# Chunk 0 of a gated attention + token-MLP kernel: V ahead of k and q, with the gate weights loaded from ScalarE's queue

## The chip, the cores and the metric

The kernel runs on one core of a Trainium2 chip. The metric is the device time of one execution in microseconds (us), as the median of several runs. Five engines work side by side, each on its own in-order list of instructions: TensorE (PE, matmuls), VectorE (DVE), ScalarE (ACT), GpSimd (POOL) and SyncE (SP, which here only starts transfers). An instruction that waits holds up everything behind it on its engine.

## The reference

One input `x` (2048 tokens x 448) goes through two branches whose results are mixed by a gate per token:

```
g = sigmoid((x * gate_w).sum(-1, keepdims=True))
a = attention(x)      # 16 heads of 28; 4 segments of 512 tokens
b = token_mlp(x)      # layernorm over 448, then mixing over the 2048 tokens
return g * a + (1 - g) * b
```

The attention branch computes `q = x @ wq`, `k = x @ wk`, `v = x @ wv`, masked softmax attention inside each of the four segments, and a linear-attention memory that each segment reads from the segments before it (`num = phi(q) @ M`, `den = phi(q) @ z`, then `M += phi(k).T @ v`). The two are mixed per head by `sigmoid(beta)` and multiplied by `wo`. The MLP branch normalizes each token, and computes `u = gelu(w1.T @ h + b1)` over tokens (2048 to 1792) and `y = w2.T @ u + b2` (1792 to 2048).

## The kernel before

**Tiling.** The 2048 tokens are 16 tiles of 128, and 4 chunks of 512 (chunk = segment). The 448 input columns are three blocks of 128 and a rest of 64. q and k of a chunk are computed transposed, in 4 head groups (`hg`) of 128 rows by 512 tokens; q and k of one head group need three matmuls of a 128-row block each (`kf`, `qf`, line 608; for chunk 0 of k one at a time, `kc`, line 618) and one of the 64-row rest (`l`, `l2`, `l3`, line 627). V is computed per token tile, with x as the stationary operand and the 448 columns of `wv` moving; a 449th column holds the gate weights, so that the gate's logits come out of V's matmuls. A tile's V is three matmuls (`vf`, line 694) and one of the rest (`vl`, `vl2`, line 706). `sc` is the scores of one fill (line 838), `exp` the softmax's exponential on ACT (line 848), `pv` the product with V (line 879). `u.f.t` is one matmul of the first MLP layer: feature tile f of 14, token tile t of 16 (line 994); `y.T.f` one of the second (line 1047); `wo` the output projection (line 1020).

**Order.** The whole order of work is written out in `PLAN` (lines 31 to 113): each item is `name.arguments@engine` and, where it has one, a buffer or PSUM bank. The items are recorded in that order, each engine's list being the items with its letter (P, A, D, G, S). A recorder (`Sched`) gives every instruction a wait on the last instruction that wrote what it reads, or that still reads what it overwrites. Nothing is reordered after that.

**Chunk 0's inputs.** `ldx.0` and `ldx.1` load the first four token tiles. Chunk 0's transposed x is made on PE (`trx`, line 552), from `ldx` and a small copy of the last 64 columns (`xw`); its results are copied out of PSUM by `ex` (line 561). Chunks 1 to 3 get their transposed x straight from DRAM (`xtd`, two transposing transfers each, lines 420 and 421) with a small copy behind it (`xtc`). Weights are loaded by `ldwk` (four transfers), `ldwq` (two) and `ldwv` (two), all on SP's queue. `pad` copies k's and q's weights into head slots of 32 columns; `rid` fills the spare columns with parts of q. `ldgw` loads the gate weights, `btg` transposes them on PE, `gcp` copies them into V's extra column in three small copies on DVE. `wvc` copies the 64-row rest of `wv`.

**Evacuation.** PSUM has 8 banks. Chunk 0's k and q are copied out by `ek` and `eq`, V by `ev` (all through `copy`, lines 367 to 371, on ACT or DVE), and the gate's logits by `gt` on ACT.

**The MLP's inputs.** Each token tile is normalized before it can be used in `u`: `bn` (statistics, DVE, line 948), `lnc` (a group of four tiles' scale and shift, ten small POOL instructions), `lna` (apply, DVE line 983 or ACT line 980). Tiles 8 to 11 come with the transfer `ldx.3`, tiles 12 to 15 with `ldx.4`. `w1` and `w2` come in 15 transfers `ldr.0` to `ldr.14` into a ring of three slots; `ldr.0` serves `u.0` and `u.1`, `ldr.2` serves `u.4` and `u.5`.

**Other transfers on SP.** `pkt` transposes the memory branch's phi(k), `gw` and `gr` send the parts of q that rode in k's spare rows through DRAM to their place; `gr` of a chunk waits for `gw` of the same chunk; `ldsm` loads the biases and beta (three transfers).

**Around the change.** Before, the recorded start is: k's weights, q's weights, V's weights, gate weights, then `xtd.1`, `ldx.2`, `xtd.2`, `ldsm`, `ldr.0`, `ldx.3`, `ldx.4`, `ldr.1`, `xtd.3` on SP; on PE twelve `kc`, then `qf` and the rests, and V of chunk 0 (`vf.0` to `vf.3`, `vl2`) after that, mixed with V of chunk 1's first half (`vl.2`, `vf.4`, `vf.5`). `l3.3` is the first PE item that needs chunk 3's transposed x.

Of the kernel before, what the change touches and what calls it, by code (L numbers as in the profile page):

```python
# [30 lines left out]
warm@P acttab@A dve0@D id@G ldx.0@S ldx.1@S mz@G ldwk.0@S ldwk.1@S ldwk.2@S ldwq@S trx.0.0@P0 xw.0@A trx.0.2@P1  # L31
trx.0.3@P xw.1@A trx.0.1@P trx.1.0@P2 ldwk.6@S trx.1.2@P3 ex.0.0@D trx.1.1@P trx.1.3@P fill@P ex.0.1@D ex.1.0@A ldwv@S
ex.1.1@A bn.3@D pad.k.0@D pad.k.1@D kc.0.3@P0 ldgw@S kc.0.2@P1 kc.1.2@P pad.k.2@D xtd.1@S kc.0.1@P0 kc.0.0@P1 kc.1.3@P
kc.1.0@P kc.1.1@P pad.q.1@D kc.2.2@P bn.2@D kc.2.0@P kc.2.1@P kc.2.3@P pad.l.1@D bn.1@D qf.0.2@P2 pad.q.0@D qf.0.3@P3
wvc@D ldx.2@S pad.l.0@D bn.0@D l2.1@P xtd.2@S qf.0.1@P2 lnc.0@G eq.0.2@A ek.0.3@D ek.0.2@A btg@P2 qf.0.0@P3 gcp@D
l2.0@P xtc.1@D pkm.0.1@D0 vl.2@P01 vf.5@P ek.0.1@A eq.0.0@D eq.0.1@A rid.q@D vf.3@P0 ev.5@A ldsm@S vf.1@P3 rid.k@D
ek.0.0@A oz@G vf.4@P rid.3@A bn.4@D ldr.0@S0 vf.0@P2 ev.4@A bn.6@D ldx.3@S vf.2@P1 bn.7@D gt.2@A eq.0.3@A vl2@P
lna.0@D l.1.2@P20 l.1.0@P13 ev.0@A ev.1@D kf.1.2@P ldx.4@S ev.2@A bn.5@D ev.3@A kf.1.0@P lna.1@D lnc.1@G gt.0@A
ek.1.2@D gt.1@A qf.1.0@P ek.1.0@A ldr.1@S1 xtc.2@D sc.0.0@P eq.1.0@D xtd.3@S l3.2@P21 exp.0.0@A0 kf.2.3@P lna.2@D
qf.1.2@P ek.2.3@D kf.1.3@P eq.1.2@D pke.0.1@A0 l.2.1@P31 ek.1.3@D sc.0.1@P kf.2.1@P lna.3@D exp.0.1@A1 pkm.0.0@D1  # L40
l.2.0@P02 bn.10@D kf.2.0@P bn.9@D qf.2.1@P bn.8@D ek.2.0@A mask.0.1@G bn.13@D qf.2.0@P eq.2.1@A bn.11@D sc.0.2@P
ek.2.1@A l.1.1@P01 eq.2.0@D lnc.2@G tb@A qf.1.1@P exp.0.2@A2 lna.4@D lna.6@D u.0.0@P3 u.0.1@P bn.14@D u.0.2@P u.0.3@P
u.1.0@P2 lna.5@D u.1.1@P lna.7@A bn.12@D u.1.2@P u.1.3@P kf.1.1@P bn.15@D pke.0.0@A1 u.0.4@P eq.1.1@D u.0.5@P u.1.4@P
ek.1.1@A u.0.6@P pkn.0.0@D u.1.5@P u.0.7@P lnc.3@G lna.8@A u.1.6@P u.1.7@P xtc.3@D pkt.0.0@S0 sc.0.3@P lna.10@D btr@P1
l3.3@P0 exp.0.3@A3 b1c@D lna.11@D u.1.8@P kf.3.3@P lna.9@D pkt.0.1@S b2c@D u.0.8@P u.0.9@P ek.3.3@D u.0.10@P u.1.9@P
u.0.11@P pkn.0.1@D sc.0.4@P vl.6@P10 exp.0.4@A4 vf.12@P pkt.0.3@S mask.0.3@G lna.12@D vf.13@P lna.13@D u.1.10@P
pkt.0.2@S ev.12@D u.0.12@P u.1.11@P ev.13@A u.0.13@P mask.0.4@G lna.14@D u.1.12@P u.1.13@P gt.6@A sc.1.0@P lna.15@A
gw.1@S l.3.1@P01 mask.0.0@G kf.3.1@P exp.1.0@A5 u.1.14@P mask.0.2@G u.1.15@P u.0.14@P qf.3.1@P eu.1@D ek.3.1@A
u.0.15@P sc.1.1@P eq.3.1@D eu.0@A pv.0@P20 ldr.2@S2 ldr.3@S0 pv.1@P01 exp.1.1@A0 ta.0@D l.3.0@P13 bet@D qf.3.0@P
u.2.0@P2 u.2.1@P u.2.2@P eq.3.0@D gr.1@S u.2.3@P sc.1.2@P kf.3.0@P pkm.1.1@D1 exp.1.2@A1 pkm.1.0@D0 u.3.0@P3 u.2.4@P  # L50
ek.3.0@D u.2.5@P u.3.1@P u.3.2@P pqm.1.0@D0 u.2.6@P u.2.7@P nr.0@D pke.1.0@A1 u.2.8@P ta.1@D sc.1.3@P mst.0@P1
exp.1.3@A2 u.3.3@P u.2.9@P msa.0@D u.2.10@P u.2.11@P u.3.4@P oa.0@D0 u.3.5@P vl.3@P01 mask.1.3@G sc.1.4@P vf.7@P
exp.1.4@A3 mask.1.2@G u.2.12@P vf.6@P ev.7@D mask.1.0@G u.3.6@P u.2.13@P ev.6@D u.2.14@P mask.1.1@G u.3.7@P u.2.15@P
gt.3@A sc.2.0@P eu.2@D l.3.2@P01 exp.2.0@A4 qf.3.2@P mask.1.4@G u.4.0@P2 u.3.8@P eq.3.2@D u.3.9@P u.3.10@P kf.3.2@P
# [193 lines left out]
def build_kernel(nc, X, WQ, WK, WV, WO, BETA, W1, B1, W2, B2, GW, OUT):  # L248
# [143 lines left out]
    def ldwv(eng, u):  # L392
        dma(eng, wvx[:, 0:3, 0:D], full3(WV), writes=[R_wv], group="wv")
        dma(eng, wvx[half[1], 3, 0:D], WV[384:448, :], writes=[R_wv], group="wv")

    def wvc(eng, u):
        copy(eng, wvx[half[0], 3, 0:D], wvx[half[1], 3, 0:D], [R_wv], [R_wv6])
# [287 lines left out]
    def vf(eng, u, t):  # L685
        tc = t // 4
        if tc == 0:
            slot["v", t] = u[0]
# [445 lines left out]
```

## Time and profile before

| | |
|---|---|
| median of 7 runs | 176.76 us (176.38 to 177.25) |
| profiled execution, its own time | 176.62 us |
| span of its trace | 174.9 us, 3285 instructions |
| PE busy | 167.5 us (96% of the span) |
| DVE, ACT, POOL busy | 133.4, 121.2, 54.3 us |
| DMA | 24.01 MB, mean 137 GB/s |
| 224 `u` and 238 `y` matmul records | 49.2 and 47.3 us |
| 40 `exp` on ACT | 75.1 us, 1877 ns each |

The profile is one execution recorded by the hardware. Starts are in us from the beginning of the span. A row's time is from its start to its modelled end; matmuls overlap, so that matmuls of 448 columns that take 353 ns by the mean start 189 ns apart. The time outside the span is 176.62 - 174.9 = 1.72 us.

### The profile page before, as it was taken

To read this page: it belongs to the slowest core of one execution; us is meant where nothing else is said; L and a number is where in the kernel's file an instruction comes from. 1 tells how busy PE (TensorE), PEld (TensorE's weight loads), DVE (VectorE), ACT (ScalarE), POOL (GpSimd) and SP (SyncE) were. 2 spreads that over 40 slices of the span, in tenths; PEclk is the share of its full clock that TensorE was granted. 3 is DMA by queue.
4 is the path that set the end of the run, shared out by engine and by line. 5 is a ranking of instruction groups with operands and counts; after the bars stand their busy time and mean duration, and the time that the engine had idled before them with its cause. 6 is when DMAs were issued, how large, how long until landed. Compare 5 with 4: busy or idle time off the path is not lost.

```text
span 174.9 us, 3285 instructions
## 1 busy us (share of the span) xinstructions
PE 167.5 (96%) x1286; PEld 78.5 (45%) x1302; DVE 133.4 (76%) x276; ACT 121.2 (69%) x113; POOL 54.3 (31%) x100
## 2 busy tenths in 40 slices
PE   7799999899999999999999999999999999999994
PEld 3334334344544444544444445444444444455563
DVE  3789969876757884899599476899998979996113
ACT  4239899688878788878997979995787774600300
POOL 7044534872075046320400009123108252200000
PEclk9999999999999999999999999999999999999999
DMA  5987999243950398189791542600727268291022
GB/s 139 261 179 155 267 340 181 60 84 83 307 146 4 47 240 105 22 223 222 193 236 27 151 95 59 185 0 0 222 72 210 74 183 225 71 250 43 2 67 64
DMA packets 49456, 24.01 MB, mean 137 GB/s; under 512 B 14337, under 2 KB 49441, under 8 KB 49441
## 3 DMA queue, kind: packets, MB, share of 16 engines
q1 hardware_dynamic: 49441, 23.81, 55.6%
q8 instruction: 10, 0.16, 0.4%
q14 instruction: 5, 0.04, 0.1%
HBM read 18.48 MB, written 2.18 MB: 118 GB/s over the span
## 4 chain that ended last, share of the span: by engine, by line
PE 76%; SPq 9%; DMA 7%; DVE 5%; issue 2%
PE t L1047 24%; PE t L994 23%; SPq L361 9%; DMA t<-in_A_x_dram 7%; PE t L1020 7%; PE t L838 6%; PE t L879 5%; PE t L694 3%; PE t L608 3%; PE t L803 2%; DVE t L948 2%; PE t L706 1%; DVE t L1005 1%; PE t L627 1%; DVE t L1056 1%
## 5 line engine op out<-in xcount | busy, mean ns | idle before, releaser
L848 ACT ACTIVATE t<-t 128x2048 bf16<-128x2048 f32 x40 | 75.1, 1877 | 20.0 <-PE t L838 19.6
L861 POOL TENSOR_SCALAR_AFFINE_SELECT t<-t 128x1024 bf16<-128x1024 bf16 (+1 forms) x40 | 37.4, 954 | 82.2 <-ACT t L848 82.2
L994 PE MATMUL t<-t 128*128 128x448 bf16 x224 | 49.2, 353 | 0.5 <-DVE t L371 0.2
L1047 PE MATMUL t<-t 128*128 128x448 bf16 (+1 forms) x238 | 47.3, 342 | 0.2 <-issue 0.2
L1047 PEld LDWEIGHTS t<-t 128*128 128x128 bf16 x238 | 22.1, 98 | 19.4 <-issue 2.8
L994 PEld LDWEIGHTS t<-t 128*128 128x128 bf16 x224 | 20.9, 98 | 22.0 <-issue 2.3
L371 DVE CAST t<-t 128x512 bf16<-128x512 f32 (+1 forms) x23 | 15.3, 670 | 6.6 <-PE t L608 4.6
L369 ACT ACTIVATE t<-t 128x512 bf16<-128x512 f32 (+5 forms) x28 | 13.9, 533 | 8.6 <-PE t L627 5.9
L1056 DVE SCALAR_TENSOR_TENSOR t<-t 128x448 bf16<-128x448 f32 (+1 forms) x17 | 10.8, 648 | 11.3 <-PE t L1047 11.2
L608 PE MATMUL t<-t 128*128 128x512 bf16 x68 | 18.0, 380 | 0.7 <-issue 0.2
L838 PE MATMUL t<-t 28*128 28x512 bf16 (+3 forms) x256 | 15.8, 301 | 0.1
L1030 ACT ACTIVATE t<-t 128x448 bf16<-128x448 f32 x9 | 6.3, 721 | 12.0 <-PE t L1020 12.0
L1020 PE MATMUL t<-t 128*128 128x448 bf16 x64 | 14.2, 352 | 0.1
L1005 DVE TENSOR_SCALAR t<-t 128x448 bf16<-128x448 f32 x12 | 8.2, 682 | 5.8 <-PE t L994 5.7
L757 ACT ACTIVATE t<-t 128x1024 bf16<-128x1024 bf16 x12 | 12.6, 1050 | 0.0
L899 DVE STREAM_TRANSPOSE t<-t 128x512 f32<-128x512 f32 x16 | 11.1, 696 | 1.3 <-PE t L879 1.3
L940 DVE STREAM_TRANSPOSE t<-t 128x512 bf16<-128x512 bf16 x16 | 10.8, 686 | 0.1
L920 DVE SCALAR_TENSOR_TENSOR t<-t 128x448 bf16<-128x448 f32 x16 | 10.7, 686 | 0.1
L838 PEld LDWEIGHTS t<-t 28*128 28x128 bf16 x256 | 4.5, 92 | 13.9 <-issue 7.1
L694 PE MATMUL t<-t 128*128 128x449 bf16 x48 | 10.7, 354 | 0.0
L948 DVE BATCH_NORM_STATS2 t<-t 128x6 f32<-128x448 bf16 x16 | 9.3, 615 | 1.4 <-DMA t<-in_A_x_dram 1.4
L879 PE MATMUL t<-t 128*32 128x512 bf16 (+3 forms) x256 | 10.3, 301 | 0.0
(77 smaller groups left out, 155.0 us busy)
## 6 DMA issues: line engine op xcount, KB each, us to landing
t<-in_B_w_dram SPq DMA_DIRECT2D x7, 1024.0 KB, 7.9
t<-in_B_w_dram SPq DMA_DIRECT2D x8, 896.0 KB, 5.3
out_dram<-t SPq DMA_DIRECT2D x15, 112.0 KB, 1.8
t<-in_A_x_dram SPq DMA_DIRECT2D x3, 448.0 KB, 7.9
t<-in_A_x_dram SPq DMA_DIRECT2D x2, 224.0 KB, 2.7
t<-in_A_wo_dram SPq DMA_DIRECT2D x4, 98.0 KB
t<-in_A_wk_dram SPq DMA_DIRECT2D x3, 112.0 KB, 3.4
t<-in_A_wq_dram SPq DMA_DIRECT2D x1, 336.0 KB, 3.3
```

The source lines that it names most:

```text
L361: op(eng, lambda e: e.dma_start(out, in_, transpose=True) if transpose else e.dma_start(out, in_), reads=reads, writes=writes, dma=True, g ...
L369: op("ACT", lambda e: e.activation(out, in_, ACT.Copy), reads=reads, writes=writes)
L371: op(eng, lambda e: e.tensor_copy(out, in_), reads=reads, writes=writes)
L608: m = e.matmul(bank(b)[:, 0:512], wkq[:, c0 + c, 128 * hg : 128 * hg + 128], xTb[:, tc % NXT, c, :], start=first and c == 0, stop=last and ...
L694: m = e.matmul(bank(b)[:, 0 : D + 1], xTb[:, tc % NXT, c, k0 : k0 + 128], wvx[:, c, 0 : D + 1], start=tc == 0 and c == 0, stop=tc > 0 and ...
L838: last = e.matmul(bank(hl)[:, c0 : c0 + w], kT[r, hg, s * 512 + j * 128 : s * 512 + j * 128 + 128], qT[r, hg, s * 512 + 128 * j : s * 512 ...
L848: op("ACT", lambda e: e.activation(punit(i).rearrange("p (a q) -> p a q", a=4), ps[:, 0:4, :], ACT.Exp, scale=SCALE), reads=R_bank[0:4], w ...
L861: op("POOL", lambda e: e.affine_select(d, d, pattern=pat, compare_op=ALU.is_ge, fill=0.0, base=0, channel_multiplier=-1), reads=[R_P[i]], ...
L879: last = e.matmul(bank(b)[32 * hl : 32 * hl + 32, 128 * j : 512], vaug[:, 4 * s + j, 32 * h : 32 * h + 32], p4[:, hl, c0 : c0 + w], start= ...
L994: op("PE", lambda e: e.matmul(bank(b)[:, 0:D], w[:, st, (ft % 2) * 128 : (ft % 2) * 128 + 128], xtile(st)[:, 0, :], start=(st == 0), stop= ...
L1020: last = e.matmul(bank(b)[:, 0:D], oT[:, hg, T * 128 : T * 128 + 128], wo_sb[:, hg, :], start=(hg == 0), stop=(hg == NHG - 1), skip_group_ ...
L1047: op("PE", lambda e, b=b, f=f, c0=c0, n=n: e.matmul(bank(b)[:, 0:n], w[:, f, c : c + 128], uT[:, f, c0 : c0 + n], start=(f == 0), stop=(f ...
```

## The change

`PLAN` is written anew from the first to the last line, and the functions are adapted to its new start. The computation is the same, with the same matmuls.

- On PE, chunk 0 starts with V by blocks: twelve `vc` (block c of token tile t) and `vl2`; then k's twelve `kc`, and q's `qf`. `btg` stands ahead of `trx`.
- V of chunk 0 goes to PSUM banks 0 to 3, and q of chunk 0 later to the same banks (`qf` takes `u[0]`, k always a bank from 4 on), so q's matmuls come behind V's evacuation.
- `ldwv` becomes four transfers of their own, recorded ahead of `ldwk` and `ldwq`; each block of `wv` has its own resource.
- `ldgw` moves from SP's queue to ACT's.
- Among the items whose engine changes at the start: `xw.0` from ACT to DVE, `ex.0.1` from DVE to ACT, `ex.1.0` and `ex.1.1` from ACT to DVE, `pad.q.0` from DVE to ACT, `xtc.1` from DVE to ACT. `gcp` stands ahead of `ex` on DVE.
- The rest of the plan is in another order too; for the items that the prediction speaks of, the lines are below.

```diff
 PLAN = """
-warm@P acttab@A dve0@D id@G ldx.0@S ldx.1@S mz@G ldwk.0@S ldwk.1@S ldwk.2@S ldwq@S trx.0.0@P0 xw.0@A trx.0.2@P1
-trx.0.3@P xw.1@A trx.0.1@P trx.1.0@P2 ldwk.6@S trx.1.2@P3 ex.0.0@D trx.1.1@P trx.1.3@P fill@P ex.0.1@D ex.1.0@A ldwv@S
-ex.1.1@A bn.3@D pad.k.0@D pad.k.1@D kc.0.3@P0 ldgw@S kc.0.2@P1 kc.1.2@P pad.k.2@D xtd.1@S kc.0.1@P0 kc.0.0@P1 kc.1.3@P
...
+warm@P ldgw@A dve0@D id@G ldx.0@S ldx.1@S acttab@A mz@G ldwv.0@S ldwv.1@S ldwv.2@S ldwv.6@S btg@P0 trx.0.2@P1 gcp@D
+trx.0.0@P2 ldwk.0@S trx.0.1@P xw.1@A xw.0@D ldwk.1@S trx.0.3@P ex.0.0@D trx.1.2@P3 trx.1.0@P0 ldwk.2@S ex.0.1@A
+trx.1.1@P trx.1.3@P fill@P ex.1.0@D ldwq@S vc.0.0@P0 ex.1.1@D vc.0.1@P1 vc.0.2@P2 bn.3@D vc.1.2@P vc.0.3@P3 ldwk.6@S
+bn.1@D vc.1.3@P vc.1.0@P vc.2.3@P wvc@D xtd.1@S vc.1.1@P vc.2.0@P pad.k.0@D vc.2.1@P vc.2.2@P pad.k.1@D vl2@P
+kc.0.0@P2 pad.k.2@D ev.3@A kc.0.3@P1 kc.1.0@P kc.0.2@P0 pad.q.0@A pad.q.1@D kc.0.1@P3 ev.2@D kc.1.1@P kc.1.2@P
+kc.1.3@P ev.0@D ldx.2@S kc.2.1@P gt.1@A kc.2.2@P pad.l.1@D kc.2.3@P ev.1@D xtd.2@S rid.3@A qf.0.3@P2 bn.2@D gt.0@A
+kc.2.0@P qf.0.2@P3 bn.0@D l2.1@P lnc.0@G qf.0.1@P0 ek.0.2@A ek.0.3@D xtc.1@A qf.0.0@P1 pad.l.0@D eq.0.3@D l2.0@P
+eq.0.2@D ldsm@S vl.2@P01 vf.5@P ek.0.0@A rid.k@D ek.0.1@A vf.4@P rid.q@D ldr.0@S0 ev.5@A ldx.3@S eq.0.0@A pkm.0.1@D0
+l.1.1@P23 bn.7@D ev.4@A kf.1.1@P eq.0.1@A bn.5@D qf.1.1@P gt.2@A bn.6@D lna.1@A ldx.4@S sc.0.0@P lna.3@D ek.1.1@A
+l.1.2@P01 xtc.2@D pkm.0.0@D1 kf.1.2@P tb@A eq.1.1@A bn.4@D ldr.1@S1 qf.1.2@P pke.0.0@A0 ek.1.2@D lnc.1@G xtd.3@S
+l.2.1@P23 lna.2@D qf.2.1@P exp.0.0@A0 lna.0@D eq.1.2@D kf.2.1@P pkn.0.0@D l3.2@P01 kf.1.3@P eq.2.1@D ek.2.1@A kf.2.3@P
+bn.11@D ek.1.3@A u.0.0@P2 bn.8@D mask.0.0@G u.0.1@P ek.2.3@A sc.0.1@P bn.10@D l.1.0@P30 exp.0.1@A1 btr@P1 bn.9@D
+qf.1.0@P b1c@D bn.15@D lnc.2@G kf.1.0@P lna.4@D u.0.2@P b2c@D lna.6@D u.0.3@P ek.1.0@A u.0.4@P eq.1.0@D u.1.0@P1
+pke.0.1@A1 u.1.1@P u.1.2@P bn.12@D u.1.3@P sc.0.2@P bn.13@D l.2.0@P30 exp.0.2@A2 u.1.4@P lna.7@D kf.2.0@P bn.14@D
+qf.2.0@P lna.5@D pkt.0.0@S0 lnc.3@G lna.8@D u.0.5@P pkn.0.1@D u.1.5@P eq.2.0@A u.0.6@P u.1.6@P lna.9@D gw.1@S ek.2.0@A
+u.0.7@P u.1.7@P u.1.8@P xtc.3@D sc.0.3@P lna.11@D l3.3@P0 gc.0@D exp.0.3@A3 u.0.8@P kf.3.3@P pqm.1.0@D0 lna.10@D
...
+u.2.3@P u.2.4@P u.2.5@P pke.1.0@A0 u.2.6@P u.2.7@P sc.1.3@P l.3.0@P21 exp.1.3@A2 qf.3.0@P pkn.1.0@D pkm.1.1@D0 u.3.4@P
+pkt.1.0@S1 u.3.5@P u.3.6@P kf.3.0@P pke.1.1@A1 mask.1.3@G u.3.7@P gr.1@S sc.1.4@P ek.3.0@D mask.1.2@G u.2.8@P
+exp.1.4@A3 u.2.9@P eq.3.0@D u.3.8@P u.3.9@P u.2.10@P msc.0@D mask.1.0@G u.2.11@P u.2.12@P ldr.2@S2 u.3.10@P u.3.11@P
...
 """
...
-    def ldwv(eng, u):
-        dma(eng, wvx[:, 0:3, 0:D], full3(WV), writes=[R_wv], group="wv")
-        dma(eng, wvx[half[1], 3, 0:D], WV[384:448, :], writes=[R_wv], group="wv")
+    def ldwv(eng, u, j):
+        if j == 6:
+            dma(eng, wvx[half[1], 3, 0:D], WV[384:448, :], writes=[R_wvu])
+            return
+        dma(eng, wvx[:, j, 0:D], WV[128 * j : 128 * j + 128, :], writes=[R_wv[j]])
...
-            slot["k", 0, hg] = u[0] if early(0, hg) else 4 + u[0]
+            slot["k", 0, hg] = 4 + u[0]
...
-            slot["q", tc, hg] = u[0] if early(tc, hg) else 4 + u[0]
+            slot["q", tc, hg] = u[0]
...
+    def vc(eng, u, c, t):
+        if c == 0:
+            slot["v", t] = u[0]
+        b = slot["v", t]
+        op("PE", lambda e: e.matmul(bank(b)[:, 0 : D + 1], xTb[:, 0, c, 128 * t : 128 * t + 128], wvx[:, c, 0 : D + 1],
+                                    start=c == 0, stop=False, skip_group_check=True),
+           reads=[R_xT[0][2 * (t // 2) + c // 2], R_wv[c], R_gw], writes=[R_bank[b]])
```

`vf` loses its branch for chunk 0.

## The prediction

> **What bounds the kernel now.** I read the engine shares first, then the busy time by stretch, then the chain of waits up to 34 us, then SP's timeline and the waits of PE.
>
> ```profile
> PE 167.5 (96%) x1286; PEld 78.5 (45%) x1302; DVE 133.4 (76%) x276; ACT 121.2 (69%) x113; POOL 54.3 (31%) x100
> ...
> PEclk9999999999999999999999999999999999999999
> ```
> ```profile
> 16.00:33.00 17.00, 15.68 (x95) 5.96 (x95) 15.14 (x32) 13.89 (x20) 8.05 (x24) 1.00 0.91 211
> 33.00:60.00 27.00, 26.37 (x240) 12.08 (x244) 19.78 (x42) 22.54 (x19) 11.28 (x18) 1.00 0.47 110
> 60.00:172.00 112.00, 111.31 (x882) 54.59 (x890) 86.77 (x171) 77.37 (x61) 27.54 (x29) 1.00 0.50 125
> ```
> Columns of the second: stretch, length, busy PE, weight loads, DVE, ACT, POOL, clock, DMA share, GB/s. From 33 us on PE is busy in 137.7 of 139 us, at full clock: there the time is PE's work, and it is the same work in the new kernel. What can change is when PE gets past the start. In 16 to 33 us the DMA engines are at 0.91 and DVE at 15.1 of 17.
>
> ```profile
> 16.53 8.72 DMA t<-in_A_x_dram
> 25.27 2.73 DVE t L948 x5
> 28.00 0.60 DVE t L371
> 28.61 0.07 SPq L361
> 28.71 3.71 DMA t<-in_A_x_dram
> 32.42 0.42 issue
> 32.84 0.37 PE t L627
> ```
> ```profile
> 6.15 0.54 SPq L361 DMA_DIRECT2D t<-in_gate_w_dram  x1
> 6.74 3.32 SPq L361 DMA_TRANSPOSE t<-in_A_x_dram  x2
> ...
> 16.05 0.43 SPq L361 DMA_DIRECT2D t<-in_B_w_dram  x1
> 16.53 3.10 SPq L361 DMA_DIRECT2D t<-in_A_x_dram  x2
> ```
> ```profile
> PE t L618 <- DVE t L371: 0.9, 1, 0.9
> ...
> PE t L627 <- DMA t<-in_A_x_dram: 0.8, 1, 0.8
> ```
> The chain does not begin on PE. SP issues transfers without a gap from 0.78 to 16.5 us (all earlier pieces of the chain are SP), `ldx.3` lands at 25.25, DVE takes five `bn`, and the transposed chunk 3 (`xtd.3`, 32.42) releases `l3.3` at 32.84 through `xtc.3`. PE had waited 0.8 us there, and 0.9 us at 5.95 for the padded weights of k. (The chain names a DVE cast ahead of `xtd.3`; by the recorded dependencies `xtd.3` needs no late DVE result, so I take those 8 us as the queue being full of `ldr.0`, `ldx.3`, `ldx.4` and `ldr.1`.)
>
> **The change, part by part.** Starts below are the old trace's axis.
>
> *V first on PE.* `vc.0.0` needs `wv` block 0, `gcp` and `ex.0.0`. Block 0 takes SP's third place (1.79 us), where k's block was, and that row says 3.4 us to landing: 5.2. The gate path: x lands at 3.49 (first `trx`), `btg` 0.17, three `gcp` 0.58, `xw.0` 0.2, `ex.0.0` 0.43: 4.9. So PE starts at about 5.35 in place of 5.95: 0.6 us gained, pads no longer in the way. The matmuls themselves are as many as before.
>
> *Gate weights on ACT.* No row has a transfer from ACT. Its issue costs ACT between nothing and the dearest early issue of SP, 0.59 us; the table load (1.28) and its first use (0.20) then end at 2.9 at the latest, before `xw.1`'s x at 4.04: hidden by x's landing. Its own landing lies between 0.7 and 3.4 us after issue (first and last of the old gate transfer), 1.5 to 4.8; I take x's 3.5. At 4.8 the V start slips to 6.2 and the gain is gone, which by the wait worked out below changes nothing at the end.
>
> *SP's list.* Ahead of `xtd.1` stood 11 transfers, now 12: the gate's is gone, V's are four in place of two. The added two at 0.48 to 0.63 each, less the gate's 0.59: +0.37 to +0.67. The transposing issues vary too: their first parts took 2.02 and 2.49 for one shape, so 0.47 less is possible: -0.1 to +0.67. I take the step in that place, 0.6. SP has no gap there, so nothing hides it: `ldx.3` lands at 25.85, `xtd.3` at 33.0.
>
> *q behind V.* q's weights go from places 6 and 7 to 10 and 11. V's last old transfer, issued at 5.62, kept DVE waiting until 9.46, so 3.8 us: q's weights at 6.2 + 3.8 = 10.0 (9.4 if bytes decide, V's old landing). Behind that wait on DVE stand `pad.q.1`, `ev.2`, `ev.0`, `pad.l.1`, `ev.1`, two `bn`. `ev.2` ends at 10.0 + 0.38 + 0.62 = 11.0, `gt.1` at 11.2; `qf.0.3`, which needs that bank, would be reached at 10.6: 0.6 lost. DVE goes on: `ev.0`, `ev.1` 1.1, small pads 0.3, `bn` 1.1, three evacuations 1.95, `rid.k` and `rid.q` 2.2 end at 17.6, and `l.1.1` waits for `rid.q`; PE would be there at 16.2 + 0.6: 0.8 lost. Without the late weights both shrink to about nothing. From 17.6 DVE has two `pkm`, four `bn`, three `lna`, `xtc.2`, `ek.1.2`, `eq.1.2`, `pkn.0.0` and `eq.2.1`, 6.8 in all, so it is free at 24.4 and idle until `ldx.3` lands.
>
> *The new first wait.* `u.0.4` needs `lna.4`. In the new DVE list `lna.4` stands behind `bn.11`, `bn.8`, `bn.10`, `bn.9` (tiles of `ldx.3`), `b1c` and `bn.15`. So: 25.85 + 2.73 (five `bn`, the chain's row) + 0.17 + 0.38 (`lna`) = 29.15; `u.0.4` at 29.2 (`ldx.4`, 1.3 behind `ldx.3`, and POOL's `lnc.1` are in time). PE's work from `vc.0.0` to `u.0.4`: V 2.8, `kc` 2.6, 14 groups of three k or q matmuls at 0.65 9.1, two `l2` 1.06, `vl.2`, `vf.5`, `vf.4` 1.45, five rests at 0.32 1.6, two `sc` 0.66, four `u` 0.76, `btr` and the joints between tile shapes 0.9: 20.9, so arrival at 26.3, with the two losses 27.7. PE waits 1.5 us, and start gain and losses all vanish in it. Behind it: thirteen `u` at 0.189, two `sc` and one `l` at 0.33 and 0.32, `kf.2.0` and `qf.2.0` 1.3, joints 0.2: 4.95. DVE in the same time has `b2c`, `lna.6`, `eq.1.0`, `bn.12`, `bn.13`, `lna.7`, `bn.14`, `lna.5`, `lna.8`, `pkn.0.1`, `lna.9`, `xtc.3`: about 0.17 + 0.31 + 0.65 + 1.1 + 0.31 + 0.55 + 0.31 + 0.31 + 0.62 + 0.31 + 0.3 = 4.95 too. So `l3.3` starts at 34.2, not 32.84: +1.36. `xtd.3` at 33.0 + 0.42 no longer decides.
>
> *The clock.* A PE wait of 1.5 us has no row: the waits shown, 0.9 at most, left the clock full. The five warm-up matmuls (2.29 us) stand 0.43 apart against 0.216 later, so a drop for as long as the first one lasted (to 4.1 us, some 3.3) would cost 1.6. Bounds 0 and 1.6; nearest the waits shown, I take 0. (The Trainium skill, "TensorE: Matmul & The Clock Gate", "What's actually happening", lets the clock fall only after an idle window of about 3.4 us; by it the sum keeps 0 here, by the upper bound it would be 1.6 more. No run yet shows a wait of this length.)
>
> *The rest.* From `l3.3` on the lists hold the same PE items but `u.1.8`, done earlier now (0.19), and 92 changes of tile shape in both. One place looks tight: `ldr.2` now follows `pkt.1.0` and `gr.1`. From `sc.1.2` on: `sc` 0.33, `exp` 1.88, `pke` 1.06, `pkn` 0.68, `pkt` 1.25, `gr` 1.8 (three of 0.4 behind one of 0.5): ldr.2 issued 7.1 us later, while PE has 13.4 us of work to `u.4.0`. 6.3 are left for a landing that takes 5.3 (the 896 KB rows, mostly alone) to 7.9 (the 1024 KB rows, mostly queued): 0 to 1.6 lost. The queue is nearly empty there, as for the former: I take 0.
>
> Sum: 1.36 - 0.19 = +1.17. The profiled execution, 176.62 (174.9 and 1.72 around it), becomes 177.8; it lies 0.14 under the median, so the median goes to **177.9**.
>
> **Rivals.**
> - *The landing stays.* The DMA engines at 0.91, not SP, could set `ldx.3`'s landing; then it is 25.25, `u.0.4` at 28.6, `l3.3` at 33.6: +0.55, 177.3. For it: the share. Against: SP's gapless issue, and only 0.7 to 0.8 share in the slices of 9 to 17 us.
> - *Not slower.* `ldx.3` lands by 24.75 or earlier, the point from which `u.0.4` is no later than 28.1 and `l3.3`, with the 0.19, costs no more than before. SP's two transposing issues at their shorter form and the cheap issues give 25.15 at the best by rows, so the 8.7 us of `ldx.3` must shrink too. If `xtd.3` came as before, 32.84 would stand and 0.19 be won: 176.6; with it 0.5 earlier too, 176.1. Against: SP's list only grew.
> - *Later still.* `ldr.2` takes 7.9 us: +1.6, 179.5; or the clock falls, the same. For it: five small transfers go right ahead of it. Against: the 5.3 rows.
>
> **How the numbers follow.** Main case, `u.0.4` waiting for the chain from a later `ldx.3` (0.7 to 1.6 slower, 177.5 to 178.4): 0.50. The landing stays: 0.12. Later still: 0.15. Not slower: 0.23, of which 0.09 faster and 0.14 same. A measurement of this kernel tells about 0.2% from no change, so faster is under 176.4 and slower over 177.1. Range 176.7 to 179.3: it leaves about one in ten out on either side. Faster 0.09, same 0.14, slower 0.77.
>
> **What would show it.** The first V matmul at about 5.35; SP's first transposing transfer at 7.3, not 6.74; a DVE wait for x ended by a `bn` at 25.85; a PE wait of 1 to 2 us before a line 998 matmul (the old 994), ended by DVE near 29.2; the rest of 64 for chunk 3 at 34.2 without a DMA wait; then PE busy as before. Wrong if `bn.11` starts before 25, if PE reaches `u.0.4` after 29, or if PE waits again near 57 us for `w1`.

## The result, and the profile after

The changed kernel takes 178.37 us by the median (before: 176.70 in the same sessions), a ratio of 1.0093 with an interval of 1.0071 to 1.0114: slower by 0.9%. The prediction was 177.9. The profiled execution took 178.21, with a span of 176.5 where the old one had 174.9, so 1.6 us have to be found.

The page's first part, and the busy time by stretch of the changed kernel (columns as in the prediction):

```profile
PE 169.0 (96%) x1290; PEld 78.5 (44%) x1302; DVE 133.3 (76%) x272; ACT 122.8 (70%) x116; POOL 55.3 (31%) x100
```
```profile
16.00:33.00 17.00, 14.92 (x86) 5.64 (x86) 15.08 (x37) 14.52 (x20) 8.55 (x27) 1.00 0.94 218
33.00:60.00 27.00, 26.18 (x239) 11.45 (x241) 19.29 (x40) 22.66 (x21) 14.72 (x27) 1.00 0.51 89
60.00:172.00 112.00, 111.28 (x874) 53.53 (x879) 85.62 (x162) 78.74 (x62) 26.13 (x28) 1.00 0.50 128
```

Against the old rows PE has lost 0.76 us in the first stretch and 0.19 in the second, and nearly nothing in the third. (The rows don't hold the whole loss, because the same work also lies later now.) So it is again a matter of the start, and of one place between 33 and 60 us. The waits of PE and the chain of waits of the changed kernel tell which:

```profile
PE t L998 <- DVE t L987: 1.2, 1, 1.2
...
PE t L626 <- DVE t L371: 0.7, 1, 0.7
PE t L998 <- DMA t<-in_B_w_dram: 0.5, 1, 0.5
...
PE t L607 <- ACT t L734: 0.2, 1, 0.2
```
```profile
16.37 8.89 DMA t<-in_A_x_dram
25.29 1.75 DVE t L952 x4
...
36.10 2.23 DVE t L987 x2
38.38 0.36 PE t L998
```

The wait of 0.8 that ended at `l3.3` by a transfer is gone. In its place stand a wait of 1.2 for DVE's `lna.4` (`u.0.4`), one of 0.5 for `ldr.2`'s weights (`u.4.0`), and the two that the prediction put down to late q weights (0.2 at `qf.0.3`, 0.7 at `l.1.1`). The chain starts as it did, with `ldx.3` on its way from 16.37 to 25.26, but goes on through DVE and POOL (the ten small instructions of `lnc`) and not through `xtd.3`. Where the waits lie, in the timeline of PE in the changed kernel (start, length, line, shape, number, and in brackets the idle time before it and what ended that):

```profile
26.75 0.54 PE L998 MATMUL t<-t 128*128 128x448 bf16 x2
28.45 1.12 PE L998 MATMUL t<-t 128*128 128x448 bf16 x5 [1.16 <-DVE t L987]
...
33.40 0.39 PE L626 MATMUL t<-t 64*128 64x512 bf16 x1
...
56.97 0.59 PE L607 MATMUL t<-t 128*128 128x512 bf16 x2 [0.16 <-issue]
58.10 1.31 PE L998 MATMUL t<-t 128*128 128x448 bf16 x6 [0.54 <-DMA t<-in_B_w_dram]
```

`l3.3` is the 33.40 row: 0.56 later than before. The other parts of the sum come from the distance between the starts of neighbouring matmuls, less the distance that the same shapes have elsewhere: 0.23 at `u.0.14` (38.38), 0.70 at `u.4.0` (0.92 from the start of the matmul before it, where 0.22 is usual; the row's idle time of 0.54 is counted from that matmul's modelled end), 0.30 at a `y` at 125.57, and the 0.19 of `u.1.8`, which is done earlier. 0.56 + 0.23 + 0.70 + 0.30 - 0.19 = 1.60: that is the whole difference. (The 0.16 `<-issue` in the row at 56.97 is no loss: of the three matmuls of `qf` only two have a record in this trace.)

Two things in the other engines' rows matter. SP's timeline of the changed kernel, and DVE and POOL near 36 us:

```profile
7.12 2.91 SPq L361 DMA_TRANSPOSE t<-in_A_x_dram  x2
...
15.89 0.43 SPq L361 DMA_DIRECT2D t<-in_B_w_dram  x1
16.37 2.94 SPq L361 DMA_DIRECT2D t<-in_A_x_dram  x2
```
```profile
36.01 2.18 POOL L865 TENSOR_SCALAR_AFFINE_SELECT t<-t 128x1024 bf16<-128x1024 bf16 x2
...
36.10 2.52 DVE L987 TENSOR_SCALAR t<-t 128x448 bf16<-128x448 bf16 x3 [0.65 <-POOL t L978]
```

SP reaches `xtd.1` 0.38 later than before, as the added transfers want it, but the two parts take 2.91 us where they took 3.32, and `ldr.0` is issued at 15.89, before the old 16.05. So `ldx.3` lands at 25.26, within 0.01 of before. (That is one execution. In four others with the same SP list up to there, those of a_ldr2, a_lna, a_warm6 and a_eq below, `ldr.0` is issued at 16.08 to 16.46 and `ldx.3` lands at 25.50 to 25.70.) And of the three `lna` at 36.10 the first two take 1.14 and 1.16 beside two of POOL's masks, where `lna` takes 0.38 to 0.40 elsewhere in this trace.

### The profile page after: what moved, and what is told of

The parts are those of the page before. It is cut to its first block, busy times and chain, and to the rows that moved or that the text cites. A ratio compares the mean times of both kernels' runs of the same rounds, so it can differ in the third digit from the quotient of the medians.

```text
span 176.5 us, 3293 instructions
## 1 busy us (share of the span) xinstructions
PE 169.0 (96%) x1290; PEld 78.5 (44%) x1302; DVE 133.3 (76%) x272; ACT 122.8 (70%) x116; POOL 55.3 (31%) x100
## 4 chain that ended last, share of the span: by engine, by line
PE 69%; SPq 10%; DMA 9%; POOL 4%; DVE 3%; issue 2%; ACT 2%; DVEq 0%
PE t L1051 25%; PE t L998 19%; SPq L361 10%; PE t L1024 7%; PE t L842 6%; DMA t<-in_A_x_dram 5%; PE t L883 5%; DMA t<-in_B_w_dram 4%; PE t L698 2%; POOL t L961 2%; PE t L807 2%; PE t L607 1%; POOL t L974 1%; DVE t L987 1%; ACT t L852 1%
## 5 line engine op out<-in xcount | busy, mean ns | idle before, releaser
L998 PE MATMUL t<-t 128*128 128x448 bf16 x224 | 50.1, 353 | 1.9 <-DVE t L987 1.2
L371 DVE CAST t<-t 128x512 bf16<-128x512 f32 (+1 forms) x25 | 16.0, 656 | 8.6 <-PE t L607 4.5
L1034 ACT ACTIVATE t<-t 128x448 bf16<-128x448 f32 x13 | 9.4, 721 | 16.3 <-PE t L1024 16.1
L369 ACT ACTIVATE t<-t 128x512 bf16<-128x512 f32 (+7 forms) x26 | 13.7, 553 | 7.8 <-PE t L710 3.1
L1024 PE MATMUL t<-t 128*128 128x448 bf16 x64 | 14.6, 352 | 0.0
L924 DVE SCALAR_TENSOR_TENSOR t<-t 128x448 bf16<-128x448 f32 x16 | 11.3, 710 | 0.0
L1009 DVE TENSOR_SCALAR t<-t 128x448 bf16<-128x448 f32 x9 | 6.1, 678 | 6.1 <-PE t L998 6.0
L961 POOL TENSOR_TENSOR t<-t 128x4 f32<-128x4 f32 x20 | 5.0, 252 | 16.6 <-DVE t L952 13.0
```

The costliest lines, as they stand in the source:

```text
L369: op("ACT", lambda e: e.activation(out, in_, ACT.Copy), reads=reads, writes=writes)
L371: op(eng, lambda e: e.tensor_copy(out, in_), reads=reads, writes=writes)
L998: op("PE", lambda e: e.matmul(bank(b)[:, 0:D], w[:, st, (ft % 2) * 128 : (ft % 2) * 128 + 128], xtile(st)[:, 0, :], start=(st == 0), stop= ...
L1024: last = e.matmul(bank(b)[:, 0:D], oT[:, hg, T * 128 : T * 128 + 128], wo_sb[:, hg, :], start=(hg == 0), stop=(hg == NHG - 1), skip_group_ ...
```

## The experiments

Each ratio is to runs of the kernel before on the same chip in the same session; "the changed kernel" is 178.37 (1.0093). Where microseconds are subtracted, they are medians of different sessions, in which the kernel before stood between 176.70 and 177.18, so a difference of a few tenths means little by itself. The items named are those of `PLAN`.

### 1. ldr.2 at its old place (a_ldr2)

```diff
-... u.0.12@P pkt.0.3@S u.0.13@P ...
+... u.0.12@P pkt.0.3@S ldr.2@S2 u.0.13@P ...
-... u.2.12@P ldr.2@S2 u.3.10@P ...
+... u.2.12@P u.3.10@P ...
```

> The changed kernel with one transfer, ldr.2 (w1 for u.4 and u.5), moved up on SP's list: right behind pkt.0.3, ahead of pkt.1.0 and gr.1, where the kernel before had it. Theory (0.7 of the 1.6 us is ldr.2 issued at 51.16 behind those two and landing at 58.05): it is issued by about 46 us, lands by about 53, the wait of 0.54 at u.4.0 ended by the DMA is gone; DVE's ta.2 ends at 57.65, so u.4.0 starts near 57.7 instead of 58.10: 0.4 to 0.7 us faster than the changed kernel, 177.7 to 178.0. Rival (the ring slot frees late, or the landing is bound by the DMA engines' other traffic, so the place on the list is not the cause): u.4.0 at 58.1 still, time unchanged within 0.2. Second rival: the earlier transfer holds up pkt.1.0 and gr.1, and a PE wait turns up behind them: no gain or a loss.

177.66, ratio 1.0046 (1.0020 to 1.0071): 0.71 less than the changed kernel. SP and PE in its timeline:

```profile
39.48 0.59 SPq L361 DMA_DIRECT2D t<-in_B_w_dram  x1
```
```profile
57.22 0.59 PE L607 MATMUL t<-t 128*128 128x512 bf16 x2 [0.16 <-issue]
57.65 1.30 PE L998 MATMUL t<-t 128*128 128x448 bf16 x6
```

`ldr.2` is issued at 39.48 and lands at 46.50; `u.4.0` follows the matmul before it without a gap, at 57.65. The theory holds, at the upper end of its range. The profiles agree: this one is 0.25 behind the changed kernel at `u.0.4` (28.70 for 28.45) and 0.45 ahead of it at `u.4.0` (57.65 for 58.10). `ldr.2` took 7.0 us to land here and 6.9 in the changed kernel, where it was issued at 51.16: not the queue around it was at fault, but that it was asked for only some 6.3 us before its use.

### 2. lna.4 and lna.6 ahead of ldx.3's statistics (a_lna)

```diff
-kf.2.3@P bn.11@D ek.1.3@A ... bn.15@D lnc.2@G kf.1.0@P lna.4@D u.0.2@P b2c@D lna.6@D
+kf.2.3@P lna.4@D lna.6@D bn.11@D ek.1.3@A ... bn.15@D lnc.2@G kf.1.0@P u.0.2@P b2c@D
```

> The changed kernel with lna.4 and lna.6 put ahead of bn.11 on DVE, so that u.0.4 no longer waits behind the statistics of ldx.3's tiles. Theory A (the wait of 1.16 us at u.0.4 is one form of a limit that POOL's chain lnc.2, lnc.3 sets behind ldx.3's landing at 25.26): the wait at u.0.4 goes and l3.3 starts near 32.6 or waits for xtd.3, but bn.11 and lnc.2 and lnc.3 end as late as before or later, so u.0.14 still starts at 38.4 or later: 0 to 0.2 us faster than the changed kernel. Theory B (the wait at u.0.4 is the loss by itself, as the prediction had it): everything behind comes 0.8 us earlier and the time falls by 0.6 to 0.9, to about 177.5.

178.89, ratio 1.0090 (1.0057 to 1.0122): no gain. DVE and PE in its timeline:

```profile
25.66 0.98 DVE L987 TENSOR_SCALAR t<-t 128x448 bf16<-128x448 bf16 x2 [1.15 <-POOL t L978]
26.57 2.19 DVE L952 BATCH_NORM_STATS2 t<-t 128x6 f32<-128x448 bf16 x4
...
29.50 0.93 PE L998 MATMUL t<-t 128*128 128x448 bf16 x4 [1.09 <-DVE t L504]
```

`lna.4` itself stood waiting for POOL's `lnc.1`, until 25.66, and held up the four `bn` behind it by 1.0 us, though `ldx.3` had landed at 25.52. `u.0.4` got what it needed, and the next `u` waited 1.09 us for `b2c`, which stands behind the same `bn` and frees a bank. Neither theory had seen that bank; of the two, A (a limit behind the wait) is nearer. The wait at `u.0.4` was one of several behind the same statistics.

### 3. ldx.3 and ldx.4 ahead of ldr.0 (a_ldx)

```diff
-rid.q@D ldr.0@S0 ev.5@A ldx.3@S eq.0.0@A ... lna.1@A ldx.4@S sc.0.0@P
+rid.q@D ldx.3@S ldx.4@S ldr.0@S0 ev.5@A eq.0.0@A ... lna.1@A sc.0.0@P
```

> The changed kernel with ldx.3 and ldx.4 ahead of ldr.0 on SP. Theory (each of these transfers lands in the order of the list, and the place decides): ldx.3 lands near 20 instead of 25.26, ldr.0 near 25.8 instead of 22.59; u.0.0, the first user of ldr.0, then waits from about 24.2 to 25.9; u.0.4 near 28.8 with a wait ended by DVE gone or small; POOL's lnc.2 and lnc.3 end 3 to 4 us earlier and the wait at u.0.14 (0.23) goes. Sum against the changed kernel: between 0.4 faster and 0.3 slower. Rival (POOL's chain matters for nothing): u.0.14 starts at the same distance behind l3.3 as it did and the time follows u.0.4 alone, 0.3 slower or more.

179.17, ratio 1.0117 (1.0083 to 1.0151): 0.8 slower than the changed kernel, worse than I had allowed. `ldx.3` lands at 20.10, as expected, and `ldr.0` at 26.34, half a microsecond later than expected. The waits at `u.0.4` and `u.0.14` are gone, but `u.0.0` now waits for `ldr.0`:

```profile
26.39 0.55 PE L998 MATMUL t<-t 128*128 128x448 bf16 x2 [1.06 <-DMA t<-in_B_w_dram]
```

It starts at 26.39 where it had started at 24.21, and from there to `l3.3` it is the same work. I had put `u.0.4` at 28.8 when 26.39 and the 2.9 us of work between give 29.3. In both orders the one of `w1` and x that comes second on this queue ends a wait of PE; the swap only chose which one.

### 4. ldsm behind ldr.0 (a_sm)

```diff
-eq.0.2@D ldsm@S vl.2@P01 ... rid.q@D ldr.0@S0 ev.5@A ...
+eq.0.2@D vl.2@P01 ... rid.q@D ldr.0@S0 ldsm@S ev.5@A ...
```

(`tb`, the only early user of `ldsm`, goes behind `exp.0.1` on ACT; `ldsm` is issued ahead of `ldx.3`.)

> The changed kernel with ldsm (three small transfers, the biases and beta) taken from ahead of ldr.0 to behind it and ahead of ldx.4 or later, so that SP issues ldr.0 and ldx.3 earlier; the table copy that needs ldsm stands behind exp.0.1 on ACT. It tells apart what sets the landing of ldx.3, which came at 25.26 although I had put it 0.6 later. Theory A (SP's issue times set it): ldr.0 is issued up to 1.5 us earlier, ldx.3 lands near 23.8, the waits at u.0.4 (1.16) and u.0.14 (0.23) shrink to nothing, l3.3 near 32.6: 0.8 to 1.1 us faster than the changed kernel, 177.3 to 177.6. Theory B (the traffic ahead of it on the DMA engines sets it): ldr.0 issued earlier, ldx.3 still lands between 25.0 and 25.4, time unchanged within 0.3.

177.52, ratio 1.0024 (0.9997 to 1.0052): 0.85 less than the changed kernel by the medians (1.2 by the ratios). SP's timeline of this kernel, and one wait of its PE:

```profile
14.84 0.58 SPq L361 DMA_DIRECT2D t<-in_B_w_dram  x1
15.47 2.64 SPq L361 DMA_DIRECT2D t<-in_B_b_dram  x2
18.15 0.42 SPq L361 DMA_DIRECT2D t<-in_A_beta_dram  x1
18.62 0.98 SPq L361 DMA_DIRECT2D t<-in_A_x_dram  x2
```
```profile
11.75 0.81 PE L607 MATMUL t<-t 128*128 128x512 bf16 x3 [1.35 <-ACT t L734]
```

Read it against the changed kernel's rows: `ldr.0` is issued 1.05 earlier and lands 1.2 earlier (21.41 for 22.59). `ldx.3` is issued 2.2 later, at 18.62, and yet lands 1.5 earlier, at 23.78. So the time of its own issue did not set its landing. It lands as the second of a train that begins with `ldr.0`'s issue: 2.4 us behind `ldr.0` here, 2.7 in the changed kernel and in the one before. (The distance is not a constant: in the profiles of a_eq, b_sm, hyb and hyb_rid below it is 1.2 to 1.6.) Theory A is right in the number, but what counts is the issue of the train's head. The waits at `u.0.4` and `u.0.14` are gone and `l3.3` starts at 33.03; waits of 1.35 at `qf.0.3` for q's weights, after a quick start (see the end), of 0.7 at `l.1.1` and of 0.6 for `ldr.2` are left.

### 5. Both transfers mended (a_sm_ldr2)

Edits 1 and 4 together.

> The changed kernel with both edits that gained alone: ldsm behind ldr.0 (0.85 us by the medians) and ldr.2 behind pkt.0.3 (0.71). Theory (two separate losses at two places, u.0.4 with u.0.14 and u.4.0): the gains add, 178.37 - 0.85 - 0.71 = 176.8, a ratio of 1.000 to the kernel before with 0.002 on either side; no wait on a DMA and none above 0.2 on DVE from 20 us on. Rival (one limit behind both, such as the DMA engines, so that the second gain is partly the first): 177.2 or more.

176.77, ratio 0.9976 (0.9951 to 1.0001): the two gains add to within 0.05 us. All the waits of PE in its profile:

```profile
PE t L476 <- PEq L1123: 0.8, 1, 0.8
PE t L626 <- DVE t L371: 0.7, 1, 0.7
PE t L554 <- DMA t<-in_A_x_dram: 0.3, 1, 0.3
```

The first is the start of the program, the last x's landing; the one between is `l.1.1` waiting for `rid.q`. With these two transfers elsewhere, the changed kernel is no slower than the one before.

### 6. The old order with ldsm behind ldr.0 (b_sm)

```diff
-rid.q@D vf.3@P0 ev.5@A ldsm@S vf.1@P3 rid.k@D ... vf.4@P rid.3@A bn.4@D ldr.0@S0 vf.0@P2 ...
+rid.q@D vf.3@P0 ev.5@A vf.1@P3 rid.k@D ... vf.4@P rid.3@A bn.4@D ldr.0@S0 ldsm@S vf.0@P2 ...
```

> The kernel before with ldsm behind ldr.0 and nothing else. It shows whether the gain of that move belongs to the new order or to the old one too. Theory (the train ldr.0, ldx.3, ldx.4, ldr.1, xtd.3 lands at the DMA engines' pace from the issue of ldr.0, in both kernels): ldr.0 issued about 1 us earlier, xtd.3 lands near 31.4 instead of 32.42, the wait of 0.78 at l3.3 goes: 0.6 to 0.8 us faster than before, ratio 0.9955 to 0.9965, near 176.1. Then the distance of the two orders, each with its transfers mended, is the worth of V first: a_sm_ldr2 against b_sm. Rival (xtd.3 is bound by its own issue of some 7.8 us): xtd.3 still at 32.4, no gain.

176.72, ratio 0.9983 (0.9957 to 1.0010): a gain of 0.3, half of what I expected, and not told from none. The mechanism is there: `xtd.3` lands at 31.46 for 32.42 and `l3.3` no longer waits. In the profiled execution the gain ends at the matmuls of `mst.1`, here and in the kernel before:

```profile
69.81 1.05 PE L802 MATMUL t<-t 128*128 128x128 bf16 x16 [0.64 <-DVE t L370]
```
```profile
69.80 1.07 PE L803 MATMUL t<-t 128*128 128x128 bf16 x16
```

PE comes there earlier and waits, and starts no sooner than before. The profile names a DVE cast, but that one had ended at 69.25; the last transposing transfer ahead of these matmuls landed at 69.61, where it had landed at 68.78 in the kernel before. Whether the other executions lose the gain there too is not known. Against experiment 5 it compares the two orders as wholes: with `ldsm` behind `ldr.0` on both sides, they stand at 0.9976 and 0.9983, and the intervals overlap almost wholly. No difference between the new order and the old can be told there. That is not the worth of V first alone, since the rest of the plan differs too.

### 7. The new start with the old order behind it (hyb)

The first part of the new `PLAN`, up to and with `eq.0.2`; then the old order, without what is done already.

> The changed kernel's first part, up to eq.0.2 (V by blocks first, gate weights on ACT's queue, k, then q behind V's evacuation), and from there on the order of the kernel before. It tells V first from the rest of the new plan. Theory (what was lost lies in the rest of the plan: lna.4 behind ldx.3's statistics, ldr.2 late): l3.3 bound by xtd.3 as before, near 32.6, u.4.0 without a wait, total within 0.2% of the kernel before, ratio 0.998 to 1.002. Rival (V first with q behind V's evacuation costs by itself, by the wait for wq at qf.0.3 of 0.4 to 1.5 us and rid.q): 0.5 us or more slower than before, ratio 1.003 or more.

179.35, ratio 1.0110 (1.0055 to 1.0165). By the numbers the rival is right, but not for its reason: no wait at `qf.0.3` above 0.4. PE's timeline, and the busy time by stretch, of this kernel:

```profile
15.62 1.32 PE L698 MATMUL t<-t 128*128 128x449 bf16 x6
18.79 0.61 PE L626 MATMUL t<-t 64*128 64x512 bf16 x4 [1.84 <-DVE t L371]
19.33 3.80 PE L607 MATMUL t<-t 128*128 128x512 bf16 x9
```
```profile
17.00:19.40 2.40, 0.61 (x5) 0.22 (x6) 2.22 (x8) 1.05 (x4) 1.14 (x8) 1.00 0.77 199
19.40:23.00 3.60, 3.60 (x9) 1.05 (x9) 2.97 (x7) 0.60 (x1) 1.32 (x6) 0.53 1.14 331
```

The rest of 64 of chunk 1's third head group waits 1.84 us, because `rid.q` and `rid.k` stand behind `pkm.0.1` and `eq.0.0` in this list. And then the mean granted clock of the next 3.6 us is 0.53 (0.50 from 19.60 to 22.90): nine matmuls in 3.80 us that take 2.12 elsewhere in the same trace. That is 1.7 us on top of the wait. Five of this kernel's six executions show a mean granted clock of 0.989 or 0.990 over the span and take 178.22 to 180.23; the sixth shows 1.000 and takes 177.79. So the hybrid does not separate V first from the rest: with the old order behind it the new start waits for `rid`, which the new plan has earlier in DVE's list.

### 8. One more warm-up matmul (a_warm6)

```diff
-NWARM = 5
+NWARM = 6
```

> The changed kernel with six warm-up matmuls of ones instead of five; they are thrown away. In three of the four experiments so far chunk 0's V ran at 374 ns per matmul until 7.2 us, in the others and in the changed kernel's profile at 189 from the start, the step to full clock being at 4.1 to 4.2 or at 7.2; the sum of PE's idle time between the warm-up and the first transposes was 0.31 to 0.40 in the slow starts, 0.26 to 0.30 in the fast ones of the new order. Theory (PE's idle time ahead of 4.2 decides the step): with the sixth matmul the idle time is below 0.15, the step is at 4.2, V ends near 8; but q then waits for wq (landing 9.5 to 10.5) and u.0.4 for ldx.3, so the time stays within 0.3 of the changed kernel, with less spread. Rival (the start decides the time): 0.5 us or more faster. Second rival (chance decides the step): it may still be at 7.2.

178.56, ratio 1.0087 (1.0055 to 1.0120): unchanged. In the profiled execution V ran at 189 to 194 ns from 5.41 on, and then `qf.0.3` waited 0.7 for q's weights, `u.0.4` 0.8 and `u.4.0` 0.8. What a quick start gained was handed to the next waits. That PE's idle time decides the step is not shown by one execution with a quick start, where the same order shows both kinds with five warm-up matmuls; it stays open.

### 9 to 11. eq.0.2 on ACT: in the changed kernel (a_eq), in the mended one (a_best), and with lna.4 earlier (a_best2)

```diff
-xtc.1@A qf.0.0@P1 pad.l.0@D eq.0.3@D l2.0@P eq.0.2@D ldsm@S
+xtc.1@A eq.0.2@A qf.0.0@P1 pad.l.0@D eq.0.3@D l2.0@P ldsm@S
```

(In the second `ldsm` is behind `ldr.0` and `ldr.2` behind `pkt.0.3`; the third also has `lna.4@D` ahead of `b1c@D`.)

> The changed kernel with one evacuation, eq.0.2, on ACT (0.55 us, into ACT's idle time near 14.5) instead of DVE, so that rid.q on DVE ends 0.6 earlier and l.1.1 no longer waits 0.71 for it. It tests the claim that what chunk 0 gains or loses ahead of u.0.4 vanishes in u.0.4's wait. Theory: the wait at l.1.1 goes, the wait at u.0.4 grows from 1.16 to 1.7 to 1.9, u.0.4 still at 28.4 to 28.7, time within 0.2 of the changed kernel (178.2 to 178.6). Rival (the wait at l.1.1 is paid for in full): 0.6 to 0.7 faster, 177.7. Third case: a PE wait of 1.84 us, in another kernel, was followed by 3.3 us of matmuls at half speed (409 to 427 ns for 216); if this wait comes to that length too, the half speed costs up to 1.6, and the kernel is slower although a wait was taken away.

178.51, ratio 1.0088 (1.0052 to 1.0123): nothing gained. The two longest waits of PE in its profile, and the row of the first:

```profile
PE t L998 <- DVE t L987: 1.3, 1, 1.3
PE t L998 <- DMA t<-in_B_w_dram: 0.8, 1, 0.8
```
```profile
28.89 1.12 PE L998 MATMUL t<-t 128*128 128x448 bf16 x5 [1.32 <-DVE t L987]
```

The 0.7 at `l.1.1` has left the list, and the wait at `u.0.4` is 1.32. Its length alone proves little: in this execution `qf.0.3` waited 0.7, and `ldx.3` landed at 25.70, 0.44 later than in the changed kernel. But in every profile in which PE waits there, `u.0.4` starts 3.19 to 3.20 behind the landing of `ldx.3`, however long PE had waited: 28.45 behind 25.26 (a wait of 1.16), 28.70 behind 25.50 (a_ldr2, 0.35), 28.84 behind 25.65 (a_warm6, 0.82), 28.89 behind 25.70 here. That is the claim of the prediction, that losses ahead of `u.0.4` vanish in its wait. After this wait of 1.32 the matmuls kept their pace.

> The changed kernel with ldsm behind ldr.0, ldr.2 behind pkt.0.3 (together 176.77) and eq.0.2 on ACT. In the kernel with the two transfers moved, u.0.4 had 0.5 us to spare behind lna.4 (ends 27.22, u.0.4 at 27.75). Theory (a wait is worth its length up to the spare of the next): the wait of 0.72 at l.1.1 goes, 0.5 of it is kept: 176.2 to 176.4, ratio to the kernel before 0.994 to 0.996. Rival (no spare behind it, something else sets the end): 176.7 still.

176.30, ratio 0.9961 (0.9931 to 0.9992). The same edit that was worth nothing is worth 0.47 here by the medians, near the 0.5 that `u.0.4` had to spare. By the ratios it is 0.0015, less than 0.3 us, and the intervals of this kernel and that of experiment 5 overlap; what speaks for it is the pair of profiles, in which `l3.3` starts 0.55 earlier (the second row is experiment 5's). No wait of PE is left but the start's:

```profile
PE t L476 <- PEq L1123: 0.8, 1, 0.8
PE t L554 <- DMA t<-in_A_x_dram: 0.3, 1, 0.3
```
```profile
32.13 0.39 PE L626 MATMUL t<-t 64*128 64x512 bf16 x1
```
```profile
32.68 0.39 PE L626 MATMUL t<-t 64*128 64x512 bf16 x1
```

> As the one before it, and lna.4 on DVE ahead of b1c and bn.15 (0.6 us earlier). Theory: the wait of about 0.2 at u.0.4 that the last edit leaves goes too: 0.2 faster than the one before it, 176.0 to 176.2. Rival (bn.15 0.3 later makes POOL's lnc.3 and with it u.0.14 late): no gain, or 0.2 slower.

176.10, ratio 0.9954 (0.9923 to 0.9985). The expected 0.2 by the medians; the intervals of the two overlap, so that it beats the one before it is not shown. Both are faster than the changed kernel and than the one before.

### 12. The hybrid with rid earlier (hyb_rid)

```diff
-eq.0.2@D pkm.0.1@D0 ... eq.0.0@D eq.0.1@A rid.q@D ev.5@A ldsm@S rid.k@D ...
+eq.0.2@D rid.k@D rid.q@D pkm.0.1@D0 ... eq.0.0@D eq.0.1@A ev.5@A ldsm@S ...
```

> The hybrid (the changed kernel's first part, then the order of the kernel before; 179.35 by the median) with rid.k and rid.q right behind eq.0.2 on DVE, ahead of pkm.0.1 and eq.0.0. In the hybrid, PE stood still for 1.84 us ahead of the rest of 64 of chunk 1's third head group, and from 19.5 to 22.9 eight matmuls of 512 columns then came 409 to 427 ns apart instead of 216: 1.7 us more. In the kernels of the changed order PE stood still for up to 1.32 us and kept its pace. Now rid.q ends near 17.6, the rest starts when ACT's gt.2 lets its bank go, near 18.3, and eq.0.0 ends near 18.6: PE's wait is some 1.3 to 1.5 instead of 1.84. Theory (the length of the wait decides, and the limit lies between 1.33 and 1.84): no half speed behind it; the kernel gains 0.4 for the wait and 1.7 for the speed, to about 177.3. Rival (the half speed has another cause, or the limit lies lower): it stays, the kernel gains 0.5 at most, to 178.9.

178.91, ratio 1.0092 (1.0060 to 1.0125). Its stretches and PE's timeline:

```profile
17.00:19.40 2.40, 1.23 (x8) 0.32 (x7) 2.27 (x8) 1.42 (x4) 1.71 (x10) 1.00 0.60 144
19.40:23.00 3.60, 2.37 (x15) 0.81 (x12) 3.59 (x9) 2.08 (x2) 1.16 (x6) 1.00 1.14 329
```
```profile
18.48 0.61 PE L626 MATMUL t<-t 64*128 64x512 bf16 x4 [1.17 <-ACT t L734]
19.02 2.12 PE L607 MATMUL t<-t 128*128 128x512 bf16 x9
...
22.69 0.39 PE L626 MATMUL t<-t 64*128 64x512 bf16 x2 [1.23 <-DVE t L371]
```

On the clock the theory is right: the wait is 1.17, the granted clock stays at 1.00, and the nine matmuls take 2.12 us. On the time it is wrong: the median fell by 0.44 and not by 2.1, because PE came 1.9 us earlier to the next rest of 64 and stood there for 1.23 us, for a cast that DVE's list gives it too late. (In this execution `qf.0.3` also waited 1.3, behind a quick start.)

## Why the prediction was right, and where its steps were off

**Right in direction and range, and near in the number partly by luck.** Slower was forecast as the likeliest, and 178.37 lies in the range. It lies in the main case, 177.5 to 178.4, by its number only: that case wanted a later `ldx.3`, and two errors of opposite sign made up for it (below). Behind the landing the chain is as said: V starts at 5.35, `u.0.4` becomes the first wait that counts, ended by DVE behind `ldx.3`'s statistics, and from it to `l3.3` it is 4.95 us to the hundredth (28.45 to 33.40).

**SP's list was mis-sized: 0.6 assumed, about 0 measured** (0.01 at `ldx.3`'s landing in the profile of the changed kernel, 0.25 to 0.45 in the four others with the same list). I had both bounds (-0.1 to +0.67) and took nearly the upper, by counting transfers. The transposing issues gave it back (2.91 us for 3.32 in `xtd.1`), and `ldr.0`, the head of the train, went out 0.16 early. Hence `ldx.3` at 25.26, not 25.85; `u.0.4` at 28.45, not 29.2 (0.6 of it by the landing; the five `bn` and `b1c` took 2.72 and not 2.90); `l3.3` 0.56 later, not 1.36. The rival "the landing stays" had the landing right (25.25), and `l3.3` nearer than the main case, at 33.6; its total of 177.3 missed for want of `ldr.2`. Its reason, the DMA engines, stays open: experiment 4 shows only that an earlier issue of `ldr.0` brings the landing forward though `ldx.3` itself is issued later.

**ldr.2 was mis-sized: 0 assumed, 0.70 measured.** The bounds of 0 to 1.6 were there; I took the bottom of them for a queue "nearly empty", by 5.3 us rows, and the landing took 6.9. So one of the signs of being wrong came true: PE waited again near 57 us for `w1`. Experiment 1 gives it back, 0.70 in the profiles and 0.71 by the medians. This error (0.70 too little) and the former (0.80 too much at `l3.3`) nearly cancel, which is luck; +1.17 became +1.60 by that and the next two.

**Not foreseen:** 0.23 at `u.0.14`, by POOL's `lnc.3` and the slow `lna` behind it (it goes with the earlier landing, experiment 4), and 0.30 at a `y` at 125.57. The latter stands in every kernel of the new order at 0.29 to 0.30; the profile names no releaser for it, and nothing here tests it.

**The waits for q's weights** were 0.4 and 0.77 by the distance of the matmuls, for 0.6 and 0.8, and the gate's issue on ACT took 0.59, the bound that was used. That they are hidden by `u.0.4` is shown by its fixed distance from the landing (a_eq); that the one at `l.1.1` is not once `u.0.4` has no wait, by the profile of a_best.

**The clock**: price 0 held in the changed kernel (a wait of 1.16 and full pace after it). The rival, half speed after a longer wait, was closer than I gave it: 1.32 us costs nothing here, 1.84 us cost 1.7, near the 1.6 that I had for it.

**What the change is worth.** Of the 1.6 us, 0.70 comes from the place of `ldr.2`, which the new plan asks for later than the old one. The wait at `u.0.4` comes from the new order itself: PE is there at 27.29, and `lna.4` lets it go at 28.45. `ldsm` stands ahead of `ldr.0` in both plans; putting it behind takes the wait away because `ldx.3` lands earlier. With both transfers moved no difference from the old order can be told (experiments 5 and 6). What V first with its own weights and queue is worth alone is not shown, as both hybrids brought waits of their own. With the two transfers, one evacuation and `lna.4` moved, the new plan makes a kernel at 0.9954 (0.9923 to 0.9985) of the one before.

## What to carry to other kernels

A wait taken away is worth no more than the spare time of the next wait behind it: cost an edit at the first place downstream that waits anyway, and look for the transfer or list that sets that place. In a queue that is always full, ask which transfer is the head of the train that the critical one rides in, and move that; as long as the critical one stays behind the head, the time of its own issue may not matter (experiment 4). Ahead of the head it does: `ldx.3` landed 5.2 us earlier in experiment 3. Of a load that moves later, compare the time to its use with the longest landing among the rows, not the shortest.

## What the runs showed of the hardware that was not expected

**Half speed after a wait of PE.** The granted clock fell to 0.50 (19.60 to 22.90) after PE had stood for 1.84 us (hyb), and stayed at 1.00 after 1.35 (a_sm), 1.32 (a_eq), 1.30 and 1.17 (hyb_rid) and 1.16 (the changed kernel). The Trainium skill ("TensorE: Matmul & The Clock Gate", "What's actually happening") has the half rate come only after an idle window of some 3.4 us; here a shorter one was enough, and the measurement decides. Where between 1.35 and 1.84 the limit lies, and whether it is a fixed one, wasn't tried.

**The start comes in two speeds.** V's matmuls in the changed kernel and in experiment 1, PE's timeline of each:

```profile
5.35 2.45 PE L688 MATMUL t<-t 128*128 128x449 bf16 x12
```
```profile
5.75 2.34 PE L688 MATMUL t<-t 128*128 128x449 bf16 x7
```

In the second the first matmuls are 374 to 377 ns apart, until about 7.2 us, in the first 189 to 194 from the beginning, for the same list of instructions on PE. Over the profiled executions the step to full speed lies anywhere from 4.1 to 7.3 us. The granted clock reads 1.00 in both, so it doesn't show this half speed; the distances of the matmuls do. The same page says that the window is free-running, so that the step depends on where in it the first matmul falls, and that it varies by 0.5 us either way. Here it varies by 3.2 us from the first to the last, and the measurement decides; that the phase of a window is the cause is not shown by a run.

**DVE beside POOL.** Two `lna` in a row take 0.69 us elsewhere in the changed kernel. Beside POOL's masks the first two of the three took 2.23 there, 2.07 in a_sm and 2.22 in the other eight kernels of the new order (not the hybrids): some three times as long. Both engines are let go by the same end of `lnc.3`, so they start together in each of these traces.

**Issue times of transposing transfers.** The second part of `xtd.1`, the same transfer in every kernel, took between 1.25 and 1.94 us to issue over these executions, the first between 1.37 and 2.10. In this stretch half a microsecond on SP can't be read from its list.
